# A two-layer network in float32 halves: the last phase's second layers by seven products of mixed blocks

## The chip, the core and the metric

The kernel runs on one core of a Trainium2 chip. The metric is the device time in microseconds of one execution, as the median of several runs; a profile is taken of one execution of its own.

## What is computed

Banded attention (4 batches of 576 positions, 8 heads of 64) gives 2304 tokens of width 512. They pass a mixture of eight experts and then one more two-layer network; the change touches the latter. Cut to what matters:

```python
for e in range(8):                       # phases 0 and 1: experts, F = 1024
    h = np.maximum(x @ w1[e], 0.0)
    out += P[:, e:e + 1] * (h @ w2[e])
...
h = x @ w_in                             # phases 2 and 3: D = 512, F = 2048
r = np.maximum(h, 0.0)
return ((r * r) @ w_out).astype(np.float32)
```

Each float32 operand is kept as a high and a low half in the fast float format, and a product is three matmuls: high by high, low by high and high by low.

## The kernel before

**Steps and phases.** The hidden width is cut in blocks of 256. A step is one such block for one set of tokens, and there are 80: phase 0 is steps 0 to 31 (experts, tokens 0 to 1279), phase 1 steps 32 to 63 (experts, tokens 1280 to 2303), phase 2 steps 64 to 71 (second network, tokens 0 to 1279), phase 3 steps 72 to 79 (second network, tokens 1280 to 2303). `first` holds the starts 0, 32, 64, 72.

**Units.** The instructions of TensorE are written in units of six matmuls of 512 columns. The first layer of step i takes seven of them, u1 to u7, seven products of mixed blocks in place of eight (`l1_pair`, L597; `product`, L533). In phases 0 and 2 a further unit of 24 half-wide matmuls does the tokens 1024 to 1279 (`l1_single`, L698), and two units their second layer. The second layer of step i runs in step i + 1, between the first layer's units: in phases 0, 2 and 3 as eight plain units of 128 tokens (`l2_units`, L722), each ended by an addition into `acc` on VectorE (L755; in the first step of a phase a copy, on VectorE or, for odd c, on ScalarE, L747); in phase 1 (`kept`, L114) as seven products v1 to v7 of mixed blocks of two banks each (`l2_mixed`, L779), whose sums stand with the width, not the tokens, on the partitions. So a step with plain second layer has 15 units in phase 3 and 18 in phase 2, one with a mixed second layer 14.

**What sets the order.** The order on each engine is written out by hand. `after(k, f)` emits f after the unit that stands k units on in the program; I call that slot k of a step. Every engine then works through its own queue in that order, and waits only where data or a buffer are missing; SyncE issues all DMAs in one such queue. The banks of PSUM named mm are three, used in turn.

**Weights.** `prep_w(i)` (L144) splits the first-layer weights of step i + 1 and the second-layer weights of step i. In phase 0 the split weights, and the mixed blocks that VectorE's and GpSimd's sums make of them, are written to DRAM (`store`, L117), and phase 1 fetches them (`fetch`, L121). In phases 2 and 3 the second-layer weights of a step are loaded to the one buffer `raw2` (`load_w`, L138), ScalarE casts the high half (slot 1), VectorE subtracts for the low half (slot 3, L156), and at once the load of the next step's is issued (L228). In step 64 these stand at slots 11 and 13. The first-layer weights go the same way through `raw1` and four GpSimd sums (L170 to L175) with `blk` at slots 2 and 5 and `sum` at slots 8 and 11. Phase 2 also turns the 64-bit input of the second network's weights into float32 (`narrow`, L234) and splits the tokens of phase 3 (`blocks_of`, L273).

**After a unit.** u4's result is copied out of its bank by ScalarE (L677) before u5 may add to that bank.

Of the kernel before, what the change touches and what calls it, by code (L numbers as in the profile page):

```python
# [30 lines left out]
KC = DM // 128  # L31
# [16 lines left out]
def tile_kernel(ctx: ExitStack, tc: tile.TileContext, a):  # L48
# [37 lines left out]
        n + h: dram.tile([NS1 + 1, 128, 1024], F32, name=f"w_{n}{h}") for n in ("blk", "sum", "w2", "mix") for h in ("h", "l")  # L86
# [27 lines left out]
    def kept(i):  # L114
        return NS1 <= i < 2 * NS1
# [28 lines left out]
    def prep_w(i):  # L144
# [52 lines left out]
        if kept(i):  # L197
            w2 = wset[i % 2]["w2"]
            out += [(0, lambda: fetch("w2", i, w2)), (0, lambda: fetch("mix", i, mixes[i % 2]))]
            if i == 2 * NS1 - 3:  # L200
                out += [(2, lambda: load_w(2 * NS1 + 1, 0)), (2, lambda: load_w(2 * NS1, 1))]
        elif 0 <= i < NS1:
            w2 = wset[i % 2]["w2"]
            m = mixes[1]
# [12 lines left out]
            at = (0, 0, 0, 1, 9, 10) if i == 0 else (1, 3, 6, 7, 13, 15)  # L217
            if i:
                out += [(at[0], hi(w2, raw2)), (at[1], lo(w2, raw2, lambda: store("w2", i, w2)))]
            out += [(at[2], m1), (at[3], m2)]  # L220
            out += [(at[4], hi(m, mix32)), (at[5], lo(m, mix32, lambda: store("mix", i, m)))]
        elif i < 0:
# [374 lines left out]
    def l1_pair(i):  # L597
# [7 lines left out]
        def made_here():  # L605
            g_t[i, 0] = tuple(
                z.rearrange("p (f n) -> p f n", f=FC) for z in (gbuf[i % 2][:, :2048], gbuf[i % 2][:, 2048:])
            )
            for n in ("s2", "s3"):
                made[n] = post[0].tile([128, 512], F32, tag=n, name=n, bufs=1)  # L610
            if i == NS1:
                r32.extend((tmp("r1"), tmp("r2"), mix32[:, :512], mix32[:, 512:], tmp("r5")))
# [9 lines left out]
        def out_mixed(fc, t, src, k):  # L622
# [3 lines left out]
            p = p_t[1, steps[i][1] // SPE, t]  # L626
# [58 lines left out]
        def u6():  # L685
            product(bank_b, i, "blk", 3, 3, stop=True)
            out(1, 0, bank_b, 1 if kept(i) else 0)

        def u7():
            product(bank_c, i, "sum", 3, 2, stop=True)  # L690
            after(0, lambda: nc.vector.tensor_tensor(out=made["s2"], in0=bank_c, in1=made["s2"], op=ALU.add))
            out(0, 1, made["s2"], 1 if kept(i) else 2)
# [5 lines left out]
    def l1_single(i):  # L698
        def unit(fcs):

            if fcs[0] == 0:
                g_t[i, 1] = tuple(sg[:, h].rearrange("p (f n) -> p f n", f=FC) for h in range(2))
            gh, gl = g_t[i, 1]
# [18 lines left out]
    def l2_units(i, which):  # L722
# [5 lines left out]
        gh, gl = g_t[i, which]  # L728
# [50 lines left out]
    def l2_mixed(i):  # L779
# [6 lines left out]
        mixed = lambda k: [z[:, k] for z in mix]  # L786
        (a0, a1), (b0, b1) = l2_banks

        def unit(banks, w, n, dst=None, start=False, stop=False, first=False, final=False):
# [11 lines left out]
            def add():  # L801
                e, t = dst
                for m, ps in enumerate(banks):
# [5 lines left out]
                    if final and s == NS1 - 1:  # L809
# [9 lines left out]
            v6=lambda: unit(b_, mixed(1), "t2", (0, 1), first=True),  # L819
            v5=lambda: unit(a_, mixed(0), "t1", (1, 1), start=True, first=True),  # L820
# [369 lines left out]
```

## Time and profile before

| | us |
|---|---|
| median of three runs | 1949.42 |
| the three runs | 1948.12, 1949.42, 1956.59 |
| profiled execution | 1946.08 |
| span of its trace, first to last instruction | 1944.3 |
| phase 2, first unit u1 of step 64 to that of step 72 | 1559.06 to 1772.72 |
| phase 3, first unit u1 of step 72 to the end | 1772.72 to 1944.3 |

Times in the trace count from the first instruction. A busy TensorE is not one at its peak, so a step is measured from the start of its first u1 to that of the next. An engine that is idle costs time only where TensorE waits for it.

### The profile page before, as it was taken

The numbers are of one execution on the slowest core, as the hardware profiler recorded it, in microseconds if no ns is written. First come the engines' busy times: TensorE is split into PE (matmuls) and PEld (weight loads), VectorE is DVE, ScalarE is ACT, GpSimd is POOL, SyncE is SP. The second block draws the span as 40 slices with busy tenths as digits, with TensorE's granted clock in tenths as the row PEclk, the third lists the DMA queues.
The fourth block names the chain that finished last, engine by engine and source line by source line (L and its number), as shares of the span: only waits on it lengthen the run. The fifth ranks groups of instructions, "written<-read, shape, count | busy, mean of one in ns | idle before, by whom it ended". The sixth has DMA issues, their size and how long they took to land.

```text
span 1944.3 us, 29199 instructions
## 1 busy us (share of the span) xinstructions
PE 1926.6 (99%) x11060; PEld 1605.6 (83%) x11060; DVE 1631.1 (84%) x2309; ACT 747.0 (38%) x1222; POOL 601.5 (31%) x532
## 2 busy tenths in 40 slices
PE   8999999999999999999999999999999999999999
PEld 7778888888888888888888888888888878888887
DVE  5867888889888888887589999999999988977776
ACT  3543433333333323333343343433334354433442
POOL 4632333234333322333124243433323331211120
PEclk9999999999999999999999999999999999999999
DMA  7665677676666665666967677675667754334111
GB/s 263 218 239 195 238 269 271 243 275 245 235 250 243 246 244 221 249 225 236 395 238 298 246 261 261 253 256 226 227 229 275 283 198 151 131 125 187 51 54 44
DMA packets 151420, 437.29 MB, mean 225 GB/s; under 512 B 15584, under 2 KB 38512, under 8 KB 151280
## 3 DMA queue, kind: packets, MB, share of 16 engines
q1 hardware_dynamic: 151280, 435.43, 60.4%
q8 instruction: 87, 1.43, 0.3%
q14 instruction: 53, 0.43, 0.1%
HBM read 257.03 MB, written 178.33 MB: 224 GB/s over the span
## 4 chain that ended last, share of the span: by engine, by line
PE 95%; DVE 4%; issue 1%; ACT 1%; POOL 0%; DVEq 0%; ACTq 0%; POOLq 0%
PE mm L738 31%; PE pt L539 16%; PE s L539 11%; PE xt L539 11%; PE mm L794 9%; PE mm L711 6%; PE s L794 3%; PE xt L794 3%; PE xt L412 1%; PE mm L904 1%; PE s L360 1%; PE pt L397 0%; DVE acc L755 0%; DVE suml L156 0%; PE mm L446 0%
## 5 line engine op out<-in xcount | busy, mean ns | idle before, releaser
L738 PE MATMUL mm<-w2h,g 128*128 128x512 f32 x1536 | 474.0, 390 | 0.2 <-DVE acc L749 0.2
L738 PEld LDWEIGHTS mm<-w2h,g 128*128 128x128 f32 x1536 | 287.4, 188 | 59.7 <-DVE acc L749 0.6
L751 DVE SCALAR_TENSOR_TENSOR acc<-mm,ptile,acc 128x512 f32<-128x512 f32 x290 | 216.9, 748 | 103.8 <-PE mm L738 103.5
L738 PE MATMUL mm<-w2l,g 128*128 128x512 f32 x768 | 298.9, 389 | 0.0
L170 POOL TENSOR_TENSOR sums<-raw 128x256 f32<-128x256 f32 x48 | 38.7, 805 | 707.5 <-DVE suml L156 682.4
L738 PEld LDWEIGHTS mm<-w2l,g 128*128 128x128 f32 x768 | 144.2, 188 | 30.2
L640 POOL TENSOR_TENSOR r<-mix,r 128x512 f32<-128x512 f32 x32 | 42.2, 1318 | 408.0 <-DVE mix L629 396.1
L619 DVE TENSOR_TENSOR g<-r,g 128x512 fp32r<-128x512 f32 x128 | 147.6, 1153 | 12.8 <-ACT g L616 4.6
L755 DVE TENSOR_TENSOR acc<-mm,acc 128x512 f32<-128x512 f32 x146 | 99.3, 687 | 56.9 <-PE mm L738 56.0
L539 PE MATMUL pt<-x_hi,sumh 128*128 128x512 f32 x320 | 124.8, 390 | 1.3 <-ACT s L677 1.3
L539 PE MATMUL s<-x_hi,blkh 128*128 128x512 f32 x320 | 125.4, 392 | 0.6 <-ACT pt L665 0.6
L539 PE MATMUL xt<-x_hi,sumh 128*128 128x512 f32 x320 | 125.0, 391 | 0.0
L539 PE MATMUL xt<-x_hi,suml 128*128 128x512 f32 x320 | 124.7, 390 | 0.1
L616 ACT CAST g<-mix 128x512 fp32r<-128x512 f32 x96 | 59.7, 622 | 169.5 <-DVE mix L629 103.2
L539 PE MATMUL s<-x_lo,blkh 128*128 128x512 f32 x320 | 124.7, 390 | 0.0
L577 ACT ACTIVATE sg<-mm 128x512 fp32r<-128x512 f32 (+1 forms) x35 | 19.7, 562 | 273.1 <-PE mm L711 273.1
L539 PE MATMUL s<-x_hi,blkl 128*128 128x512 f32 x320 | 124.6, 389 | 0.0
L539 PE MATMUL pt<-x_lo,sumh 128*128 128x512 f32 x320 | 124.5, 389 | 0.0
L539 PE MATMUL pt<-x_hi,suml 128*128 128x512 f32 x320 | 124.5, 389 | 0.0
L539 PE MATMUL xt<-x_lo,sumh 128*128 128x512 f32 x320 | 124.5, 389 | 0.0
L808 DVE TENSOR_TENSOR acc<-mm,acc 128x512 f32<-128x512 f32 x188 | 120.2, 680 | 0.0
L711 PE MATMUL mm<-xs,blkh 128*128 128x256 f32 x640 | 115.8, 280 | 0.0
(202 smaller groups left out, 4646.1 us busy)
## 6 DMA issues: line engine op xcount, KB each, us to landing
raw<-in_w SPq DMA_DIRECT2D x61, 512.0 KB, 5.8
w_blkh<-blkh SPq DMA_DIRECT2D x33, 512.0 KB, 6.1
w_blkl<-blkl SPq DMA_DIRECT2D x33, 512.0 KB, 6.5
w_sumh<-sumh SPq DMA_DIRECT2D x33, 512.0 KB, 6.7
w_suml<-suml SPq DMA_DIRECT2D x33, 512.0 KB, 2.6
blkh<-w_blkh SPq DMA_DIRECT2D x33, 512.0 KB, 3.3
blkl<-w_blkl SPq DMA_DIRECT2D x33, 512.0 KB, 4.2
sumh<-w_sumh SPq DMA_DIRECT2D x33, 512.0 KB, 4.5
```

The lines of the kernel that those rows point to most:

```text
L170: tt(out=c(sums, 0), in0=c(raw1, 2), in1=c(raw1, 3), op=ALU.add)
L539: nc.tensor.matmul(ps, w[:, c], z[:, x, j], start=start and k == 0, stop=stop and k == 5, skip_group_check=True)
L577: after(k, lambda: nc.scalar.activation(out=ghi, in_=src, func=AF.Relu))
L616: after(k, lambda: nc.scalar.copy(b[:, 0], src))
L619: lambda: nc.vector.tensor_tensor(out=b[:, 1], in0=src, in1=b[:, 0].bitcast(F32), op=ALU.subtract),
L640: sub = lambda o, x, y: nc.gpsimd.tensor_tensor(out=o, in0=x, in1=y, op=ALU.subtract)
L711: nc.tensor.matmul(ps[:, n * NSG:n * NSG + NSG], w[:, c], z[:, kc], start=k == 0, stop=k == 3 * KC - 1)
L738: nc.tensor.matmul(ps, g[:, fc, c * 128:c * 128 + 128], wt[:, fc], start=k == 0, stop=k == 3 * FC - 1)
L751: nc.vector.scalar_tensor_tensor(out=dst, in0=ps, scalar=p, in1=dst, op0=ALU.mult, op1=ALU.add)
L755: nc.vector.tensor_tensor(out=dst, in0=ps, in1=dst, op=ALU.add)
L794: nc.tensor.matmul(ps, w[wt][:, c], z[:, g], start=start and k == 0, stop=stop and k == 2, skip_group_check=True)
L808: nc.vector.tensor_tensor(out=o, in0=ps, in1=o, op=ALU.add)
```

## The change

The second layers of steps 72 to 78 go by seven products of mixed blocks, as in phase 1. For that, phase 2 writes the split weights of its steps to DRAM: `blk`, `sum`, `w2`, and the four mixed blocks of `w2`. The mixed blocks are made in place in `raw2` by four GpSimd sums (m3, m4), their high half goes to a buffer of its own, their low half back to `raw2`, both are stored from there, and only then is the next step's `raw2` loaded. Phase 3 fetches all this in place of loading and splitting weights. The weight cast of step 65 moves from slots 1 and 3 to 9 and 11; in steps 66 to 71 it stays at 1 and 3. The relu of two of the four blocks is written out by ScalarE first, and VectorE's product follows one slot later. The second layer of step 79 stays plain. As the sums of phase 3 now stand turned, 32 transposes (eight sets of four) turn them back between its eight units.

```diff
     def kept(i):
-        return NS1 <= i < 2 * NS1
+        return NS1 <= i < 2 * NS1 or i >= first[3]
+
+    def mixed(i):
+        return kept(i) and i < len(steps) - 1
+
+    def place(i):
+        return i % NS1 if i < first[2] else NS1 + (i - first[2]) % NS2
 
...
-        if NS1 < n <= 2 * NS1:
+        if NS1 < n <= 2 * NS1 or first[3] <= n < len(steps):
...
             def keep(name):
                 if n == 0:
                     kept_back.append(lambda: store(name, 0, w[name]))
-                elif n <= NS1:
-                    store(name, n, w[name])
+                else:
+                    store(name, NS1 if n == NS1 else place(n), w[name])
...
         if kept(i):
             w2 = wset[i % 2]["w2"]
-            out += [(0, lambda: fetch("w2", i, w2)), (0, lambda: fetch("mix", i, mixes[i % 2]))]
+            out += [(0, lambda: fetch("w2", i, w2))]
+            if mixed(i):
+                out += [(0, lambda: fetch("mix", i, mixes[i % 2]))]
...
+            def m3():
+                tt(out=r[:, 1, 1], in0=r[:, 0, 1], in1=r[:, 1, 1], op=ALU.add)
+                tt(out=r[:, 0, 1], in0=r[:, 0, 0], in1=r[:, 0, 1], op=ALU.subtract)
+
+            def m4():
+                tt(out=r[:, 0, 0], in0=r[:, 1, 1], in1=r[:, 0, 0], op=ALU.subtract)
+                tt(out=r[:, 1, 0], in0=r[:, 1, 0], in1=r[:, 0, 0], op=ALU.subtract)
+
+            if moe:
+                at = (0, 0, 0, 1, 9, 10) if i == 0 else (1, 3, 6, 7, 13, 15)
+            else:
+                at = {first[2]: (11, 13, 14, 14, 19, 20), first[2] + 1: (9, 11, 12, 12, 16, 17)}.get(i, (1, 3, 4, 5, 9, 11))
             if i:
-                out += [(at[0], hi(w2, raw2)), (at[1], lo(w2, raw2, lambda: store("w2", i, w2)))]
+            if moe:
+                out += [(at[2], m1), (at[3], m2)]
+                out += [(at[4], hi(mixes[1], mix32)), (at[5], lo(mixes[1], mix32, lambda: store("mix", place(i), mixes[1])))]
+            elif i + 1 < first[3]:
+                m = (mixes[1][0], raw2.bitcast(F32R))
+
+                def mix_done():
+                    store("mix", place(i), m)
+                    load_w(i + 1, 1)
+
+                out += [(at[2], m3), (at[3], m4), (at[4], hi(m, raw2)), (at[5], lo(m, raw2, mix_done))]
...
-        else:
-            w = wset[i % 2]
-            at = (11, 13) if late else (1, 3)
-            out += [(at[0], hi(w["w2"], raw2)), (at[1], lo(w["w2"], raw2, lambda: load_w(i + 1, 1)))]
...
+            if i == len(steps) - 1:
+                pair = {(0, 0): block["11"], (1, 1): block["21"], (1, 0): block["t2"], (0, 1): block["t1"]}
+                g_t[i, 0] = {k: (z[:, 0], z[:, 1]) for k, z in pair.items()}
...
-            p = p_t[1, steps[i][1] // SPE, t]
+            moe = steps[i][0]
+            if moe:
+                p = p_t[1, steps[i][1] // SPE, t]
+            elif (fc, t) in ((0, 0), (1, 0)):
+                p = post[0].tile([128, T], F32, tag="pp", name="pp", bufs=3)
+                after(k, lambda: nc.scalar.activation(out=p, in_=src, func=AF.Relu))
+                k += 1
+            else:
+                p = src
             after(
                 k,
                 lambda: nc.vector.scalar_tensor_tensor(
@@ -631,11 +666,11 @@
                 ),
             )
             if (fc, t) == (0, 0):
-                operand("11", g, 1, 2)
+                operand("11", g, k + 1, k + 2)
...
             elif (fc, t) == (1, 0):
-                operand("21", g, 2, 3)
+                operand("21", g, k + 1, k + 2)
...
             k = 0
+            t, c0 = divmod(c, T // 128)
             for fc in range(FC):
+                gh, gl = g_all[fc, t]
                 for g, wt in ((gh, whi), (gl, whi), (gh, wlo)):
                     nc.tensor.matmul(
-                        ps, g[:, fc, c * 128:c * 128 + 128], wt[:, fc], start=k == 0, stop=k == 3 * FC - 1
+                        ps, g[:, c0 * 128:c0 * 128 + 128], wt[:, fc], start=k == 0, stop=k == 3 * FC - 1
                     )
                     k += 1
+            if i == len(steps) - 1:
+                o, ch = by_token[c], t0 // 128 + c
+
+                def add():
+                    nc.vector.tensor_tensor(out=o, in0=ps, in1=o, op=ALU.add)
+                    nc.sync.dma_start(out[ch * 128:(ch + 1) * 128], o)
+
+                after(1 if c == 0 else 0, add)
+                return
...
+        if i == len(steps) - 1:
+            d = acc[0].rearrange("p (k t n) -> p k t n", k=KC, t=2)
+            flat = [z.rearrange("p b c -> p (b c)") for z in (raw1, sums)] + [raw2, mix32]
+            by_token = [z[:, h * DM:h * DM + DM] for z in flat for h in range(2)]
+
+            def by_tokens(c):
+                ps = bank("s")
+                t, c0 = divmod(c, T // 128)
+                for kc in range(KC):
+                    nc.tensor.transpose(
+                        ps[:, kc * 128:kc * 128 + 128], d[:, kc, t, c0 * 128:c0 * 128 + 128], ident
+                    )
+                nc.scalar.copy(by_token[c], ps)
+
+            units, turns = ([lambda c=c, f=f: f(c) for c in range(2 * T // 128)] for f in (unit, by_tokens))
+            return [units[0], turns[0]] + [u for k in range(1, len(units)) for u in (turns[k], units[k])]
+
...
+        places = range(4) if steps[i][0] else (3, 0, 1, 2)
+        mixed_w = lambda k: [z[:, places[k]] for z in mix]
...
-            l2 = [] if kept(i - 1) else l2_units(i - 1, 0)
+            l2 = [] if mixed(i - 1) else l2_units(i - 1, 0)
...
+            if i in (NS1 + 1, first[3] + 1):
                 s0, s1 = bank("s"), bank("s")
...
-                elif i == first[2] - 1:
+                elif i in (first[2] - 1, len(steps) - 1):
                     names = "u1 v1 u2 v2 u3 u4 v6 u5 v5 u6 u7 v7 v3 v4"
...
-                    after(min(k, len(order) - 1), f)
+                    after(k if k > 18 else min(k, len(order) - 1), f)
...
-                splits.append(blocks_of(2, y_dram[:, :, PAIRS[1]:], y1 + two(mixes[1][0])))
+                splits.append(blocks_of(2, y_dram[:, :, PAIRS[1]:], y1 + two(mixes[1][1])))
```

## Rows read from the trace of the kernel before

**Rows 1.** Page, part 1: an engine's busy time, share of the span, instructions.

```profile
PE 1926.6 (99%) x11060; PEld 1605.6 (83%) x11060; DVE 1631.1 (84%) x2309; ACT 747.0 (38%) x1222; POOL 601.5 (31%) x532
```

**Rows 2.** Windows by step: length, busy by engine, clock, DMA share, GB/s.

```profile
1516.82:1535.86 19.04, 19.04 (x85) 15.77 (x84) 17.28 (x26) 6.96 (x12) 6.31 (x4) 1.00 0.58 221
1578.26:1605.65 27.39, 26.59 (x127) 21.83 (x126) 24.85 (x32) 15.28 (x25) 10.82 (x10) 1.00 0.43 157
...
1631.94:1657.92 25.98, 25.98 (x128) 21.99 (x127) 23.38 (x37) 11.40 (x18) 3.65 (x4) 1.00 0.47 152
...
1684.17:1710.15 25.98, 25.98 (x128) 21.99 (x127) 24.95 (x36) 11.88 (x19) 7.52 (x8) 1.00 0.38 132
1710.15:1737.21 27.06, 26.28 (x129) 21.92 (x127) 21.13 (x31) 10.84 (x17) 3.66 (x4) 1.00 0.22 69
...
1807.16:1827.56 20.40, 20.40 (x92) 16.89 (x90) 13.85 (x20) 9.46 (x15) 3.21 (x4) 1.00 0.15 51
```

**Rows 3.** Timeline of PE between phases 0 and 1: start, length, instruction.

```profile
939.18 0.60 PE L767 MATMUL mm<-ident,acc 128*128 128x128 f32 x4
939.53 0.70 PE L738 MATMUL mm<-w2h,g 128*128 128x512 f32 x2
...
940.99 0.60 PE L767 MATMUL mm<-ident,acc 128*128 128x128 f32 x4
```

**Rows 4.** Timeline of ACT in steps 65 and 68.

```profile
1591.81 0.62 ACT L280 CAST mixh<-mix 128x512 fp32r<-128x512 f32 x1
...
1594.36 0.59 ACT L747 COPY acc<-mm 128x512 f32<-128x512 f32 x1
...
1660.49 1.06 ACT L152 CAST w2h<-raw 128x1024 fp32r<-128x1024 f32 x1
...
1663.57 0.59 ACT L677 COPY s<-pt 128x512 f32<-128x512 f32 x1
```

**Rows 5.** Timeline of PE, u5 of steps 68 and 70; in brackets the wait.

```profile
1664.73 0.39 PE L539 MATMUL pt<-x_hi,sumh 128*128 128x512 f32 x1
...
1717.91 0.50 PE L539 MATMUL pt<-x_hi,sumh 128*128 128x512 f32 x1 [0.78 <-ACT s L677]
```

**Rows 6.** Timeline of DVE in steps 64, 65 and 67.

```profile
1576.80 1.22 DVE L156 TENSOR_TENSOR w2l<-raw,w2h 128x1024 fp32r<-128x1024 f32 x1
...
1587.40 1.22 DVE L156 TENSOR_TENSOR blkl<-raw,blkh 128x1024 fp32r<-128x1024 f32 x1
...
1598.46 1.21 DVE L156 TENSOR_TENSOR suml<-sums,sumh 128x1024 fp32r<-128x1024 f32 x1
...
1649.99 1.22 DVE L156 TENSOR_TENSOR suml<-sums,sumh 128x1024 fp32r<-128x1024 f32 x1
```

**Rows 7.** Timeline of POOL, step 69: first and last of four sums.

```profile
1703.58 0.73 POOL L170 TENSOR_TENSOR sums<-raw 128x256 f32<-128x256 f32 x1 [15.46 <-DVE suml L156]
...
1706.23 1.07 POOL L175 TENSOR_TENSOR sums<-raw,sums 128x256 f32<-128x256 f32 x1
```

**Rows 8.** Timeline of SP's DMA issues in phase 0.

```profile
647.20 0.32 SPq L119 DMA_DIRECT2D w_suml<-suml  x1
...
649.16 0.32 SPq L119 DMA_DIRECT2D w_mixl<-mixl  x1
```

**Rows 9.** DMA issues, 645 to 655 us: size, median us from issue to landing.

```profile
w_suml<-suml SPq DMA_DIRECT2D x1, 512.0 KB, 2.6
w_mixh<-mixh SPq DMA_DIRECT2D x1, 512.0 KB, 3.6
w_mixl<-mixl SPq DMA_DIRECT2D x1, 512.0 KB, 5.0
```

**Rows 10.** DMA issues, 1577 to 1579.5 us, same columns.

```profile
raw<-w SPq DMA_DIRECT2D x1, 512.0 KB, 3.3
```

**Rows 11.** DMA issues, 656 to 668 us, beside seven other transfers.

```profile
raw<-in_w SPq DMA_DIRECT2D x2, 512.0 KB, 6.1
...
w_w2l<-w2l SPq DMA_DIRECT2D x1, 512.0 KB, 6.2
```

More of the change, by code (lines that the diff above doesn't have):

```diff
@@ L85, in tile_kernel @@
     w_dram = {
-        n + h: dram.tile([NS1 + 1, 128, 1024], F32, name=f"w_{n}{h}") for n in ("blk", "sum", "w2", "mix") for h in ("h", "l")
+        n + h: dram.tile([NS1 + NS2, 128, 1024], F32, name=f"w_{n}{h}") for n in ("blk", "sum", "w2", "mix") for h in ("h", "l")
     }
@@ L605, in made_here @@
         def made_here():
[L606 to L608 removed]
+            if i == len(steps) - 1:
+                pair = {(0, 0): block["11"], (1, 1): block["21"], (1, 0): block["t2"], (0, 1): block["t1"]}
+                g_t[i, 0] = {k: (z[:, 0], z[:, 1]) for k, z in pair.items()}
+            else:
+                gh, gl = (z.rearrange("p (f n) -> p f n", f=FC) for z in (gbuf[i % 2][:, :2048], gbuf[i % 2][:, 2048:]))
+                g_t[i, 0] = {(f, t): tuple(z[:, f, t * T:t * T + T] for z in (gh, gl)) for f in range(FC) for t in range(2)}
             for n in ("s2", "s3"):
                 made[n] = post[0].tile([128, 512], F32, tag=n, name=n, bufs=1)
[L611 to L612 removed]
+            if i in (NS1, first[3]):
+                r32[:] = (tmp("r1"), tmp("r2"), mix32[:, :512], mix32[:, 512:], tmp("r5"))
         def operand(n, src, k, k_lo):
@@ L686, in u6 @@
             product(bank_b, i, "blk", 3, 3, stop=True)
-            out(1, 0, bank_b, 1 if kept(i) else 0)
+            out(1, 0, bank_b, 1 if mixed(i) else 0)
         def u7():
@@ L691, in u7 @@
             after(0, lambda: nc.vector.tensor_tensor(out=made["s2"], in0=bank_c, in1=made["s2"], op=ALU.add))
-            out(0, 1, made["s2"], 1 if kept(i) else 2)
+            out(0, 1, made["s2"], 1 if mixed(i) else 2)
             if steps[i][0] and steps[i][1] % SPE == SPE - 1:
@@ L698, in l1_single @@
     def l1_single(i):
+        whole = []
         def unit(fcs):
             if fcs[0] == 0:
-                g_t[i, 1] = tuple(sg[:, h].rearrange("p (f n) -> p f n", f=FC) for h in range(2))
-            gh, gl = g_t[i, 1]
+                whole[:] = [sg[:, h].rearrange("p (f n) -> p f n", f=FC) for h in range(2)]
+                g_t[i, 1] = {(f, 0): tuple(z[:, f] for z in whole) for f in range(FC)}
+            gh, gl = whole
             ps = (spare[0] if i == 2 * NS1 else bank("mm"))[:, :len(fcs) * NSG]
@@ L808, in add @@
                         nc.vector.tensor_tensor(out=o, in0=ps, in1=o, op=ALU.add)
-                    if final and s == NS1 - 1:
+                    if final and steps[i][0] and s == NS1 - 1:
                         t0 = PAIRS[1] + t * T
@@ L818, in l2_mixed @@
             v2=lambda: unit(a_, whole(1, 0), "21", (0, 0), stop=True, first=True, final=True),
-            v6=lambda: unit(b_, mixed(1), "t2", (0, 1), first=True),
-            v5=lambda: unit(a_, mixed(0), "t1", (1, 1), start=True, first=True),
-            v7=lambda: unit(b_, mixed(2), "t3", (1, 1), final=True),
-            v3=lambda: unit(a_, mixed(3), "22", (0, 1), stop=True, final=True),
+            v6=lambda: unit(b_, mixed_w(1), "t2", (0, 1), first=True),
+            v5=lambda: unit(a_, mixed_w(0), "t1", (1, 1), start=True, first=True),
+            v7=lambda: unit(b_, mixed_w(2), "t3", (1, 1), final=True),
+            v3=lambda: unit(a_, mixed_w(3), "22", (0, 1), stop=True, final=True),
             v4=lambda: unit(b_, whole(1, 1), "t4", (1, 0), stop=True, first=True, final=True),
@@ L1042, in tile_kernel @@
                 ahead, l2, l2s = l2[:len(l2) - 3] + l2s, l2[len(l2) - 3:], []
-            if i == NS1 + 1:
+            if i in (NS1 + 1, first[3] + 1):
                 s0, s1 = bank("s"), bank("s")
                 x0, x1 = bank("xt"), bank("xt")
-                own.update((k, (s0, bank_p, x0)) for bank_p in [bank("pt")] for k in range(i, 2 * NS1))
-                l2_banks.extend(((bank("mm"), bank("mm")), (s1, x1)))
+                until = 2 * NS1 if i < 2 * NS1 else len(steps)
+                own.update((k, (s0, bank_p, x0)) for bank_p in [bank("pt")] for k in range(i, until))
+                l2_banks[:] = ((bank("mm"), bank("mm")), (s1, x1))
                 spare.append(bank("mm"))
@@ L1051, in tile_kernel @@
             l1s = l1_single(i) if pair_of(i) == 0 else []
-            if kept(i - 1):
+            if mixed(i - 1):
                 v = l2_mixed(i - 1)
```

21 lines of the change are left out of this document (8 added, 13 removed).

## Prediction

> **What bounds the kernel now.** I read the page's busy shares first, then windows cut at the steps. TensorE is busy 99% of the span [rows 1], and in the steps of phases 1 and 3 a window is as long as its PE busy time, at full clock [rows 2]: 19.04 us for a mixed step of 14 units, 20.40 us for a plain one of 15, so 1.36 us a unit. Phase 2 is the place with little room: a step there is 25.98 us with VectorE busy 23.4 to 25.0 of it, and the first and one late step have lost 1.4 and 1.1 us already (27.39 and 27.06 against 25.98) [rows 2]. So a unit less in phase 3 is worth its full 1.36 us, and anything late in phase 2 is seen at once. Nothing can be won beyond the units removed and the few microseconds that phase 2 loses today.
>
> **Part 1, phase 3.** The second layers of seven steps, 72 to 78, go from eight units to seven. These run in steps 73 to 79: 7 x 1.36 = 9.52 us less. I take the whole of it, since the mixed step of phase 1 has the same DMA fetches, adds and GpSimd sums and runs at 19.04 us with VectorE busy 17.28 and ScalarE 6.96 [rows 2]. Phase 3 adds two relus of about 0.6 us to ScalarE, which has 12 us free, and moves two products on VectorE a slot later; I put that at nothing. If that cover fails, it is a rival (E). The preparation of weights that leaves phase 3 is worth nothing, since VectorE was busy 13.85 of 20.40 us there.
>
> **Part 2, the turning back.** Eight sets of four transposes stand between the last eight units. Phase 0's end shows the same form: from the set at 939.18 to the unit at 939.53 is 0.35 us, and that unit takes until 940.99, 1.46 us in place of 1.36 [rows 3]. So 0.45 us a set, 3.6 us in all. The ScalarE copies (0.59 us each, as those of L747 [rows 4]) and two banks keep pace with one set per 1.8 us. The tail behind the last unit (one addition, one DMA) stays. Sum of parts 1 and 2: -9.52 + 3.6 = -5.9 us.
>
> A set of four costs 0.45 us, so one costs 0.11 us [rows 3]. The Trainium skill, page "TensorE: Matmul & The Clock Gate", section "Part 4: PE-mode transpose", gives some 275 ns for one in a kernel; by an estimate from that figure 32 would be 8.8 us and the sum of these two parts -0.7 us. The row is of the same instruction in this kernel, so I keep 3.6.
>
> **Part 3, phase 2: a loop through one buffer.** This decides. Before, `raw2` is free as soon as VectorE has subtracted the low half (slot 3). Now it is cast, subtracted, mixed by four GpSimd sums, cast again, subtracted again at slot 11, stored, and only when that store has landed does SyncE issue the load of the next step's weights. ScalarE meets that load at slot 1 of the next step, and what is queued behind the cast on ScalarE is the copy of u4's bank, without which u5 can't start.
>
> *The deadline.* In step 68, begun at 1657.92, the cast starts at 1660.49, the copy ends at 1663.57 + 0.59 = 1664.16, u5 starts at 1664.73 [rows 4, 5]. So the cast may be 0.57 us late: it must start by 3.14 us into the step. Step 70 shows what comes else: u5 waited 0.78 us for that copy [rows 5].
>
> *The loop in a settled step.* In step 67, begun at 1631.94, `sum`'s subtraction starts 18.05 us in and ends at 19.27 [rows 6]. The GpSimd sums new in this step take 3.7 us for four, by the row of 1703.58 to the end of that at 1706.23 [rows 7], and VectorE pays for them: step 69 with POOL at 7.52 us has VectorE at 24.95, step 67 with 3.65 has 23.38 with a like count of instructions, 1.6 us for 3.9 [rows 2]. That is for a full overlap; before slot 11 I take 1.0 us (bounds 0 and 3.7). So the store of `suml` goes out about 20.3 us in, then those of `mixh` and, 1.2 us later, `mixl`. Phase 0 issues these three in the same order within 2 us: from `suml` at 647.20 to the landing of `mixl` at 649.16 + 5.0 is 7.0 us [rows 8, 9]. A load on an emptied queue lands after 3.3 us [rows 10]. 20.3 + 7.0 + 3.3 = 30.6 us, and the next step begins at 25.98, so the weights are there 4.6 us into it: 1.5 us after the deadline. Steps 68, 69 and 70 pay this; 67 about 0.5, since the stall of step 66 has let VectorE catch up with the units; 71 about 1.0, since step 70 has little narrowing (VectorE 21.13 us [rows 2]). That is 6.0 us, less the 1.1 us that step 70 loses today at the same copy: 4.9. Bounds: nothing, if stores land in the 2.6 us of one alone [rows 9]; 5 us a step if store and load take 6.2 and 6.1 us as in the fullest stretch of phase 0 [rows 11].
>
> *Step 65.* It starts late in the loop: step 64's mixed blocks are subtracted at slot 5 of step 65, ahead of the `blk` subtraction that now starts at 1587.40; that is 1.2 us, where the weight subtraction of slot 3 has gone, so about 1589 [rows 6]. Store alone 2.6, load 3.3 [rows 9, 10]: 1595. ScalarE reaches the cast at slot 9 at 1592.4 (the end of the row at 1591.81), waits to 1595 and then casts, so the copy out of the bank at 1594.36 is some 3.6 us later [rows 4]. Three banks give 2.7 us of room; the rest and VectorE's own delay make about 2.0 us, between 0 and 6.
>
> *Step 66.* The low half of step 65's weights then comes behind `sum`'s subtraction (1598.46, now 1.6 us later, and 1.2 long [rows 6]) and is done near 1602.4; four sums of 1 us, a cast of 1.05, a subtraction of 1.2: 1608.7; mixed-store landing 3.1 (between 2.6 and 3.6), load 3.3: 1615.1. Step 66 begins near 1607.7, its deadline is 1610.8, so TensorE waits about 4.3 us (0 to 9).
>
> Phase 2 in all: 2.0 + 4.3 + 4.9 = 11.2 us more. Other additions there are at nothing: eight stores of 512 KB per step into a queue busy 0.38 to 0.47 of the time [rows 2] (a full queue is rival C), and ScalarE's extra cast of 1.05 us with half its time free.
>
> **Sum.** -5.9 + 11.2 = +5.3 us. On the profiled execution, 1946.08: 1951.4. The median of the runs shown, 1949.42, lies 3.3 us above that execution, so I give 1955.
>
> **Rivals.**
> A, the forecast: the loop through `raw2` misses its deadline by a little in most steps, 1955 (1949 to 1961).
> B, the weights are back in time: hidden. Landings at the short end, 2.6 and 3.3 us, remove the wait in steps 67 to 71 and most of steps 65 and 66, and the 1 to 3 us that phase 2 loses today may go too. For it: the queue is half empty. Against it: three stores stand before the load. -5.9 + 1.5 = -4.4, 1945 (1939 to 1948).
> C, slower: the round trip is longer, because the stores of `w2`, `blk` and `sum` share the queue. From the fullest stretch [rows 11] half the excess over my values, 2 us a step in seven steps: +14, 1969. It turns the sign beyond what I call no change when the round trip is 0.6 us longer than I took in each of the seven.
> D, VectorE becomes the bound in steps 65 to 69: it is busy 24.95 of 25.98 us in step 69 and gets 1.2 us and up to 3.9 us of collision with GpSimd [rows 2]; 1.5 us more in five steps, +7: 1962. In the Trainium skill, page "SBUF — State Buffer", section "Who interferes with whom", a VectorE instruction with two inputs in SBUF and a GpSimd one that reads SBUF lock each other out whole; by an estimate from the rule four sums of 0.9 us would cost 3.7 us a step. The rows show 1.6 for 3.9, so half of it at most.
> E, phase 3 does not reach 19.04 us a step, because the relu of u6 and the product behind it come a slot later: half the gain is gone, +4.8: 1960.
>
> **Chances.** A 0.45, B 0.25, C 0.15, D 0.10, E 0.05. The likeliest gives 1955. For 8 in 10 the range must hold A, nearly all of B and half of C and D: 1943 to 1967. What a measurement here can tell from no change is about 0.5%, 9.7 us: faster (under 1939.7) only at the low end of B, 0.04; slower (over 1959.1): C, half of D and E, a fifth of A, 0.31; within, 0.65. The gain's ceiling, 5.9 us and 3 of today's waits, is why "faster" is so small.
>
> **What would show it.** Right: steps 73 to 79 at 19.04 us; eight gaps of 0.45 us in the last eight units; u5 of step 66 waiting 3 to 5 us and of steps 68 to 70 1 to 2 us, each for the copy at ScalarE behind a cast that a DMA released. Wrong: the cast of slot 1 without idle time before it (B); landings over 6 us for `mixl` (C); TensorE waiting for VectorE's additions rather than ScalarE's copy (D); steps over 19.1 us in phase 3 (E).

## The result and the profile after

| | before | after |
|---|---|---|
| median of the runs, us | 1949.66 (1945.92 to 1956.59) | 1961.90 (1959.39 to 1963.71) |
| profiled execution, us (its span) | 1946.08 (1944.3) | 1962.93 (1961.2) |

The ratio is 1.0061, 95% interval 1.0042 to 1.0079: 12 us slower, where 1955 was forecast (1943 to 1967). The page's first part shows TensorE with 10 instructions fewer than in [rows 1] and 98% busy instead of 99%:

```profile
PE 1928.1 (98%) x11050; PEld 1602.0 (82%) x11050; DVE 1660.0 (85%) x2337; ACT 747.1 (38%) x1238; POOL 647.0 (33%) x556
```

Windows of steps 65 to 70 and of two steps of phase 3, columns as in [rows 2]:

```profile
1581.63:1616.02 34.39, 28.19 (x127) 22.97 (x126) 25.13 (x32) 17.19 (x27) 15.95 (x15) 0.95 0.89 328
1616.02:1647.77 31.75, 28.19 (x128) 22.98 (x127) 27.20 (x37) 12.70 (x20) 15.23 (x14) 0.95 0.74 263
1647.77:1674.68 26.91, 26.27 (x128) 21.91 (x127) 24.90 (x38) 12.02 (x19) 7.85 (x8) 1.00 0.79 288
1674.68:1702.04 27.36, 26.56 (x129) 21.85 (x128) 25.19 (x36) 12.65 (x20) 10.10 (x9) 1.00 0.81 286
1702.04:1729.32 27.28, 26.53 (x129) 21.82 (x128) 26.15 (x36) 12.73 (x20) 12.90 (x12) 1.00 0.79 287
1729.32:1756.84 27.52, 26.58 (x129) 21.84 (x128) 23.14 (x33) 11.48 (x18) 4.13 (x4) 1.00 0.57 226
1825.51:1844.55 19.04, 19.04 (x86) 15.77 (x85) 17.32 (x24) 8.77 (x16) 6.63 (x4) 1.00 0.62 219
1844.55:1864.09 19.54, 19.33 (x85) 15.69 (x84) 18.91 (x26) 7.91 (x14) 6.32 (x4) 1.00 0.59 216
```

Step 65 took 27.39 us before and step 67 25.98 [rows 2]. The DMA share (last column but one), 0.38 to 0.47 in steps 65 to 69 of [rows 2], is now 0.74 to 0.89 in steps 65 to 69. TensorE's idle times, from its timeline (start, length, instruction, in brackets the wait ahead of it): one row each of step 65, step 66, a settled step of phase 2 and a step of phase 3.

```profile
1605.98 1.05 PE L776 MATMUL mm<-w2h,g 128*128 128x512 f32 x2 [5.05 <-ACT acc L794]
1626.07 0.50 PE L563 MATMUL pt<-x_hi,sumh 128*128 128x512 f32 x1 [3.08 <-ACT s L710]
1668.98 0.73 PE L776 MATMUL mm<-w2h,sg 128*128 128x512 f32 x2 [0.64 <-DVE acc L802]
1871.49 0.50 PE L859 MATMUL s<-g,mixh 128*128 128x512 f32 x1 [0.21 <-DVE g L646]
```

The terms of the sum, forecast and measured (lengths from a step's first matmul to the next step's):

| term | forecast | measured |
|---|---|---|
| step 65 | +2.0 | 34.39 - 27.39 = +7.0 |
| step 66 | +4.3 | 31.75 - 26.29 = +5.5 |
| steps 67 to 71 | +4.9 | +0.9, +1.1, +1.3, +0.5, 0 = +3.8 |
| steps 73 to 79 | -9.5 | 135.90 - 143.24 = -7.3 |
| last eight units | +3.6 | 15.14 - 10.65 = +4.5 |
| sum | +5.3 | +13.4 |

The two profiled executions differ by 16.85 us. 3.35 of it lie ahead of step 0, in code that is the same, and 0.1 behind the last unit. Such differences ahead of the change are in every single execution (step 64 starts between 1557 and 1569 us), so the experiments are read by their steps and not by their totals; each but the last is one execution. Of the twelve runs of the last, e12, one took 3223 us at a mean granted clock of 0.555 and is left out of its ratio.

### The profile page after: what moved, and what is told of

The parts are those of the page before. It is cut to its first block, busy times and chain, and to the rows that moved or that the text cites. A ratio compares the mean times of both kernels' runs of the same rounds, so it can differ in the third digit from the quotient of the medians.

```text
span 1961.2 us, 29450 instructions
## 1 busy us (share of the span) xinstructions
PE 1928.1 (98%) x11050; PEld 1602.0 (82%) x11050; DVE 1660.0 (85%) x2337; ACT 747.1 (38%) x1238; POOL 647.0 (33%) x556
## 4 chain that ended last, share of the span: by engine, by line
PE 88%; DVE 8%; ACT 1%; issue 1%; DMA 1%; POOL 0%; DVEq 0%; ACTq 0%; POOLq 0%
PE mm L776 26%; PE pt L563 16%; PE s L563 10%; PE xt L563 10%; PE mm L859 10%; PE mm L747 5%; PE s L859 4%; PE xt L859 4%; DVE g L646 2%; PE xt L436 1%; PE mm L969 1%; DVE acc L873 1%; PE s L384 1%; DVE acc L802 1%; PE pt L421 0%
## 5 line engine op out<-in xcount | busy, mean ns | idle before, releaser
L776 PE MATMUL mm<-w2h,g 128*128 128x512 f32 x1312 | 407.7, 392 | 5.1 <-ACT acc L794 5.1
L776 PEld LDWEIGHTS mm<-w2h,g 128*128 128x128 f32 x1312 | 246.1, 189 | 56.0 <-ACT acc L794 5.5
L776 PE MATMUL mm<-w2l,g 128*128 128x512 f32 x656 | 256.2, 391 | 0.0
L675 POOL TENSOR_TENSOR r<-mix,r 128x512 f32<-128x512 f32 x39 | 51.8, 1328 | 551.8 <-DVE mix L664 539.8
L646 DVE TENSOR_TENSOR g<-r,g 128x512 fp32r<-128x512 f32 x156 | 182.0, 1169 | 14.2 <-ACT g L643 5.4
L873 DVE TENSOR_TENSOR acc<-mm,acc 128x512 f32<-128x512 f32 x226 | 144.6, 677 | 1.8 <-PE mm L859 1.8
L776 PEld LDWEIGHTS mm<-w2l,g 128*128 128x128 f32 x656 | 123.7, 189 | 26.0
L643 ACT CAST g<-mix 128x512 fp32r<-128x512 f32 x117 | 72.7, 622 | 187.3 <-DVE mix L664 108.5
L601 ACT ACTIVATE g<-s 128x512 fp32r<-128x512 f32 x96 | 59.6, 621 | 137.0 <-DVE s L715 69.5
```

The costliest lines, as they stand in the source:

```text
L601: after(k, lambda: nc.scalar.activation(out=ghi, in_=src, func=AF.Relu))
L643: after(k, lambda: nc.scalar.copy(b[:, 0], src))
L646: lambda: nc.vector.tensor_tensor(out=b[:, 1], in0=src, in1=b[:, 0].bitcast(F32), op=ALU.subtract),
L675: sub = lambda o, x, y: nc.gpsimd.tensor_tensor(out=o, in0=x, in1=y, op=ALU.subtract)
L776: nc.tensor.matmul(ps, g[:, c0 * 128:c0 * 128 + 128], wt[:, fc], start=k == 0, stop=k == 3 * FC - 1)
L873: nc.vector.tensor_tensor(out=o, in0=ps, in1=o, op=ALU.add)
```

## Experiments

Steps in us, and in the last column steps 73 to 79 together:

| run | 65 | 66 | 67 | 68 | 69 | 70 | 65 to 70 | 73 to 79 |
|---|---|---|---|---|---|---|---|---|
| before | 27.39 | 26.29 | 25.98 | 26.25 | 25.98 | 27.06 | 158.95 | 143.24 |
| after | 34.39 | 31.75 | 26.91 | 27.36 | 27.28 | 27.52 | 175.21 | 135.90 |
| e1 load first | 28.12 | 31.74 | 26.92 | 27.38 | 27.29 | 27.55 | 169.00 | 135.82 |
| e2 no sums | 28.68 | 28.12 | 26.76 | 27.30 | 26.80 | 27.53 | 165.20 | 135.89 |
| e3 block slot | 34.97 | 32.34 | 26.90 | 27.38 | 27.31 | 27.48 | 176.38 | 133.95 |
| e5 turn order | 35.23 | 32.06 | 26.89 | 27.36 | 27.31 | 27.48 | 176.33 | 135.89 |
| e6 two buffers | 29.51 | 29.47 | 27.52 | 27.37 | 27.72 | 29.14 | 170.73 | 135.82 |
| e7 slot 15 | 30.05 | 28.31 | 26.80 | 26.30 | 28.80 | 31.29 | 171.55 | 135.89 |
| e7b slot 9 | 29.32 | 29.99 | 27.17 | 27.94 | 27.21 | 29.27 | 170.90 | 135.82 |
| e8 all four | 29.02 | 28.71 | 26.81 | 26.25 | 28.84 | 29.71 | 169.34 | 133.97 |
| e9 early chain | 30.55 | 27.38 | 26.90 | 27.37 | 27.28 | 27.56 | 167.04 | 135.88 |
| e10 square | 30.92 | 28.16 | 27.64 | 28.16 | 28.16 | 27.65 | 170.69 | 133.93 |
| e11 slots | 28.21 | 26.63 | 26.84 | 26.41 | 27.45 | 29.79 | 165.33 | 133.94 |
| e12 best | 28.25 | 26.64 | 26.76 | 26.44 | 26.94 | 27.56 | 162.59 | 133.97 |

**e1, the load ahead of the store.**

```diff
-                m = (mixes[1][0], raw2.bitcast(F32R))
+                m = (mixes[1][0], mixes[0][0])
                 def mix_done():
-                    store("mix", place(i), m)
                     load_w(i + 1, 1)
+                    store("mix", place(i), m)
```

> The load of the next step's second-layer weights no longer waits for the store of the mixed pieces: their low half goes to a free buffer, and the load is issued ahead of that store. Theory (store and load in series through one buffer cause the long idle times of TensorE): the 5.05 us in step 65 and the 3.08 us in step 66 fall below 1 us each, the granted clock stays at 1.00 behind them, step 65 takes about 28 us and step 66 about 27, steps 67 to 70 stay at 26.9 to 27.5 because VectorE sets them; 1951 us in all. Rival (a full DMA queue, not the order): the load itself then lands after 6 us or more, TensorE still idles over 2 us in step 65, about 1957. Rival (the prediction's cast at slot 1 in steps 67 to 70): these steps fall to about 26.0 as well, 1946.

In the changed kernel the chain of step 65 reads as follows: issue of the store, its landing in the rows of DMA issues (last number, us), issue of the load, and the cast on ScalarE that waits for it; the copy that empties TensorE's bank stands behind that cast.

```profile
1592.54 0.32 SPq L125 DMA_DIRECT2D w_mixl<-raw  x1
...
w_mixl<-raw SPq DMA_DIRECT2D x1, 512.0 KB, 6.7
...
1599.28 0.80 SPq L144 DMA_DIRECT2D raw<-w  x2
...
1603.36 1.04 ACT L158 CAST w2h<-raw 128x1024 fp32r<-128x1024 f32 x1 [5.91 <-DMA raw<-w]
```

With the load first, the same cast and the wait of u5 in step 66:

```profile
1596.04 1.06 ACT L158 CAST w2h<-raw 128x1024 fp32r<-128x1024 f32 x1 [0.78 <-DMA raw<-w]
...
1617.71 0.80 PE L563 MATMUL pt<-x_hi,sumh 128*128 128x512 f32 x1 [3.15 <-ACT s L710]
```

Step 65: the idle 5.05 us are gone and the step is 6.3 us shorter; the theory holds there, and the full queue alone makes a short wait only (the load took 5.6 us, and the cast waited 0.78). Step 66: the theory fails, 31.74 against 31.75. The mixed subtraction of step 65 now ends 2.27 us into step 66 (1609.84), where in the changed kernel it ends 0.4 us in, because the stall of step 65 had let the chain catch up; so the 2.6 us of the store's landing that e1 takes out of the chain are lost again, by its later start (1.9 us) and a load that lands after 4.3 us in place of 3.4. Steps 67 to 70 do not move at all, so what they lose has nothing to do with the load.

**e2, GpSimd's sums left out**, on top of e1 (the calls of `m3` and `m4` removed).

> As the run before, but GpSimd's four sums of the second-layer weights in phase 2 are left out, so that the mixed pieces stored are not mixed; the two casts and two subtractions remain. Theory (VectorE is slowed by GpSimd's sums beside it): steps 67 to 70 fall by about 1 us each to 25.98 to 26.3, VectorE's busy time per step by 1.0 to 1.6 us; some 4 us less than the run before. Rival (VectorE's own second subtraction of 1.2 us is the cause): steps 67 to 70 stay within 0.3 us of the run before.

Steps 67 to 70 lose only 0.16, 0.08, 0.49 and 0.02 us, and the wait in front of the single's unit stays (0.48, 0.74 and 0.49 us in steps 67 to 69). Step 67 in e1 and in e2, columns as in [rows 2] (VectorE's busy time is 24.90 and 24.13 us, GpSimd's 7.86 and 4.58):

```profile
1639.31:1666.22 26.91, 26.28 (x128) 21.92 (x127) 24.90 (x38) 12.02 (x19) 7.86 (x8) 1.00 0.79 285
```

```profile
1634.57:1661.33 26.76, 26.28 (x129) 21.92 (x128) 24.13 (x38) 12.11 (x19) 4.58 (x4) 1.00 0.80 282
```

VectorE's busy time falls by 0.77 us and the step by 0.16; in steps 68 to 70 VectorE's falls by 0.51, 0.32 and 1.08. So the collision is there, smaller than expected, and it is not what sets most of these steps; in step 69 it may be a part of it. Step 66, with a chain shorter by four sums, goes to 28.12: it is the length and start of the chain that makes step 66 late.

**e6, e7, e7b: a buffer for the raw weights, and the slot of the subtraction.** In e6, from step 65 on, the load goes to `mixes[0][0]`, the sums read it and write `raw2`, and the next load is issued right behind the sums; step 65's cast is back at slot 1. e7 moves the mixed subtraction of steps 66 to 70 from slot 11 to 15, e7b to 9 (the cast to 7).

```diff
+        if which and i > first[2]:
+            dst = mixes[0][0].bitcast(F32)
...
-                tt(out=r[:, 1, 1], in0=r[:, 0, 1], in1=r[:, 1, 1], op=ALU.add)
+                tt(out=q[:, 1, 1], in0=r[:, 0, 1], in1=r[:, 1, 1], op=ALU.add)
...
+                if i > first[2]:
+                    load_w(i + 1, 1)
```

> From step 65 on the raw second-layer weights go to a buffer of their own, and the four sums read it and write the old one, so the next load waits for the sums alone and no longer for cast, subtraction and store of the mixed pieces; step 65's cast is back at slot 1. Theory (step 66 is late because the load for it waits for the end of step 65's late chain, not for the queue): the idle time of 3.1 us in step 66 goes, and the low clock behind it; step 65 takes 27.4 to 28.1 us, step 66 26.3 to 27.3, steps 67 to 70 stay at 26.9 to 27.5; about 1950 us. Rival (VectorE has too much work around step 66): step 66 stays over 29 us, with TensorE waiting for VectorE; about 1953.

> As the run before, and in steps 66 to 70 the subtraction of the mixed pieces stands at slot 15 in place of 11, where the subtraction of the sums stands too. Theory (two subtractions of 1.2 us back to back in one slot make an addition late, and with it a bank of TensorE): the idle times of 0.48, 0.64, 0.80 and 0.75 us in steps 67 to 70 go, these steps take 26.0 to 26.4 us and step 70 about 27.0; some 3 us less than the run before. Rival (VectorE has no room left in these steps, wherever the subtraction stands): the idle times come back at another unit and the steps stay at 26.9 to 27.5.

> As the run with two buffers, and in steps 66 to 70 the cast of the mixed pieces stands at slot 7 and their subtraction at slot 9, ahead of that of the sums at 11. Theory (only the same slot is the trouble): steps 67 to 70 at 26.0 to 26.4 us as with slot 15. Rival (VectorE is still behind at slot 11 when it has done one more subtraction since slot 6): the idle times stay at 0.5 to 0.8 us.

All three fell short: 170.7 to 171.6 us for the six steps, against 169.0 in e1. e6's step 66 (29.47, with waits of 1.05, 0.73 and 0.77 us) is on its rival's side. e7b takes the single's wait away in steps 66 to 69 but has another of 0.55 us, for an addition, in step 68 (27.94). But the three separate two things. VectorE's rows in step 67 of the changed kernel, ahead of the wait of 0.64 us at 1668.98:

```profile
1665.98 1.22 DVE L162 TENSOR_TENSOR suml<-sums,sumh 128x1024 fp32r<-128x1024 f32 x1
1667.11 1.22 DVE L162 TENSOR_TENSOR raw<-raw,mixh 128x1024 fp32r<-128x1024 f32 x1
1668.24 0.68 DVE L802 TENSOR_TENSOR acc<-mm,acc 128x512 f32<-128x512 f32 x1
```

Two subtractions of slot 11 stand back to back, and the addition that frees the bank comes behind both. With slot 15 that wait is gone in all of steps 66 to 69 (steps 67 and 68 at 26.80 and 26.30). (The four waits of 0.48, 0.64, 0.80 and 0.75 us that the expectations name are those of steps 66 to 69; step 70 waits 0.93 us at u5, as before with 0.78 [rows 5].) In its place u5 waits in steps 69 and 70 for ScalarE's copy, which stands behind a cast that waited for VectorE. In e7's step 70 (begun at 1722.56), first TensorE's row, then GpSimd's first sum, then one of VectorE's operations of the narrowing, and below it the same sum and the same operation in e1's step 70 (begun at 1720.90):

```profile
1732.93 0.50 PE L570 MATMUL pt<-x_hi,sumh 128*128 128x512 f32 x1 [3.39 <-ACT s L717]
...
1724.94 0.74 POOL L229 TENSOR_TENSOR raw<-mixh 128x256 f32<-128x256 f32 x1 [5.00 <-DMA w_mixl<-raw]
...
1726.00 1.11 DVE L295 SCALAR_TENSOR_TENSOR xb<-xb 128x512 f32<-128x512 uint32 x1
```

```profile
1727.64 0.73 POOL L226 TENSOR_TENSOR raw<-raw 128x256 f32<-128x256 f32 x1 [9.46 <-DVE w2l L162]
...
1722.68 0.69 DVE L288 SCALAR_TENSOR_TENSOR xb<-xb 128x512 f32<-128x512 uint32 x1
```

In e1 the sums write over what the low half reads, so GpSimd has to wait for that subtraction; with a buffer of its own GpSimd no longer waits for it, and its sums meet the narrowing that decides the start of the step. Taking a wait from GpSimd moved its work to a worse place. The buffer is only a part of it: in step 70 u5 waits 0.92 us in e1, 2.56 in e6 with the subtraction still at slot 11, and 3.39 in e7.

**e9, step 64's chain early**, on top of e1.

```diff
-                at = {first[2]: (11, 13, 14, 14, 19, 20), first[2] + 1: (9, 11, 12, 12, 16, 17)}.get(i, (1, 3, 4, 5, 9, 11))
+                at = {first[2]: (6, 7, 7, 7, 10, 13)}.get(i, (1, 3, 4, 5, 9, 11))
```

> As the run with the load ahead of the store, and step 64 casts, subtracts and sums its second-layer weights at slots 6 and 7 and the mixed pieces at 10 and 13, in the idle time that VectorE and GpSimd have there; so step 65's weights are loaded at slot 13 of step 64 as in the kernel before, and step 65 keeps to the slots of the later steps. Theory (step 66's 3.1 us come from the late start of the chain in step 64, handed on from step to step): the idle time in step 66 falls below 1 us with no low clock behind it, step 65 takes 27.4 to 28.1 us, step 66 26.3 to 27.3; steps 67 to 70 stay at 26.9 to 27.5. Rival (VectorE sets steps 65 and 66 as well, so an earlier chain only moves the wait): the two together stay over 57 us, as they did with two buffers (59.0).

Step 66 is at 27.38 without an idle row at u5: its wait was the late start of the chain, handed on from step 64. Step 65 is worse than expected (30.55: 1.59 us at u5 and 0.95 at the single's unit), since its cast, at slot 1 again and so ahead of u4's copy, waited 1.93 us for the load. The two are 57.9 together, over the 57 that the rival named: a part of the wait did move, from step 66 to step 65.

**e10, squares on ScalarE**, on top of e9 and with the edits of e3 and e5: g = Square(relu) in place of VectorE's product for three of the four blocks in phase 2.

> As the run before, with the edits of phase 3 and of the turns that each stood alone; and in phase 2 three of the five squares of a step are made by ScalarE from its own relu instead of by VectorE's product, some 2.0 us off VectorE per step. Theory (VectorE's work just ahead of the single unit sets steps 67 to 70): their idle times of 0.5 to 0.8 us go, these steps take 26.0 to 26.4 us, step 70 up to 27.0; phase 3's steps at 19.04; 12 us or more below the changed kernel and 4 to 7 below the kernel before. Rival (it is the two subtractions back to back that make one addition late, however little VectorE has to do ahead of them): the idle times stay.

The rival was right, and more than that: the waits grew.

```profile
1689.06 0.68 DVE L805 TENSOR_TENSOR acc<-mm,acc 128x512 f32<-128x512 f32 x1
1689.66 1.21 DVE L162 TENSOR_TENSOR suml<-sums,sumh 128x1024 fp32r<-128x1024 f32 x1
1690.79 1.22 DVE L162 TENSOR_TENSOR mixh<-raw,mixh 128x1024 fp32r<-128x1024 f32 x1
...
1692.66 0.72 PE L779 MATMUL mm<-w2h,sg 128*128 128x512 f32 x2 [1.22 <-DVE acc L805]
```

VectorE now had idle times of 1.83 and 0.77 us, waiting for casts that ScalarE made later, and the pair of subtractions came 19.4 us into step 68 (begun at 1670.22), in the changed kernel 18.7. So less work on VectorE did not shorten these steps. As ScalarE was slower here too, e10 alone doesn't show that the order in front of one addition sets them; e7 and e11 do.

**e11 and e12, the slots alone**, on e9 (and so e1), with e3 and e5: the mixed subtraction at slot 13 in place of 11, two slots behind the other; in e11 step 65's cast at slot 5, behind u4's copy, and its mixed subtraction at 14, in e12 also those of steps 69 and 70. The line of e12:

```diff
+                at = {64: (6, 7, 7, 7, 10, 13), 65: (5, 7, 8, 8, 12, 14), 69: (5, 7, 8, 8, 12, 14), 70: (5, 7, 8, 8, 12, 14)}.get(i, (1, 3, 4, 5, 9, 13))
```

> The load ahead of the store (in-place sums as in the changed kernel), step 64's chain early, step 65's cast at slot 5 (behind the copy that its fifth unit needs) with the mixed subtraction at 14, and in steps 66 to 70 the mixed subtraction at slot 13, two slots behind that of the sums; phase 3's earlier block and the order of the turns; squares as in the changed kernel. Theory (what delays a bank is two subtractions back to back, and what delays a cast is where it stands, not the amount of VectorE's work): steps 67 to 70 at 26.0 to 26.5 us (70: 27.0), step 65 about 28, step 66 about 26.7, so steps 65 to 70 take some 161 us against 158.95 before and 175.2 in the changed kernel; about 4 us below the kernel before. Rival (VectorE has no room, and the wait comes back as a late copy at the fifth unit, as with slot 15 and two buffers): steps 69 and 70 at 28 us or more, the six steps over 165.

> As the run before, with steps 69 and 70 laid out like step 65 (cast of the second-layer weights at slot 5, behind the copy that the fifth unit waits for; mixed subtraction at 14). Theory (the copy is late because the cast of 1.05 us stands ahead of it on ScalarE): the idle times of 0.64 us in step 69 and 1.85 us in step 70 fall by about 1 us, so that neither has a low clock behind it; step 69 about 26.8, step 70 about 27.6, steps 65 to 70 together 162 to 163 us. Rival (VectorE is late for the single's product as well, so that the cast is not what decides): step 70 stays over 29. In all 118.2 and less in steps 73 to 78 plus the turns: 3 to 4 us below the kernel before, a ratio of 0.998; at worst 1.000.

e11: there is no wait in front of the single's unit in steps 66 to 70 any more, and steps 65 to 68 come nearly as the theory has them; step 69 waits 0.64 us at u5, and step 70 is the rival's, with u5 1.85 us late, as are the six steps together (165.33). e12: with the cast behind the copy, step 69 is 26.94 and step 70 27.56. The 1.29 us that u5 still waits in step 70 are VectorE's, as the rival has it: another cast ahead of that copy waited 3.01 us for the product of the single's unit, behind the narrowing. The six steps take 162.59 us, 12.6 less than in the changed kernel and 3.6 more than before. From step 65 to the end e12 is 1.4 us shorter than the kernel before, by these two executions, where 3 to 4 us were expected; the measured ratio is 1.0002 (0.9990 to 1.0013; medians 1947.54 of 12 runs and 1946.95 of 17). The change, repaired, is worth nothing that can be measured. Step 67 still takes 0.78 us more than before without an idle time of 0.15 us or more on TensorE; where that goes is not shown.

**e3, phase 3's block one slot earlier.**

```diff
-            out(1, 0, bank_b, 1 if mixed(i) else 0)
+            out(1, 0, bank_b, 1 if mixed(i) and steps[i][0] else 0)
```

> In phase 3 the relu, product, cast and subtraction of hidden block (1, 0) come one slot earlier, where phase 1 has them. Theory (the low half of that block now falls beside GpSimd's sums, 1.78 us in place of 0.68, and makes the low halves of the mixed blocks late): steps 75 to 78 go from 19.54 to 19.59 back to 19.04, about 2.5 us in all, 1959.5. Rival (the slower low halves have another cause, such as the pair of relus): the 0.2 us idle in each step stays, 1961.9.

Steps 74 to 79 at 19.04 each; 1.95 us for the seven steps, where 2.5 were expected. The low half of that block in the changed kernel, beside GpSimd's sum (POOL, its second of four), and in e3, ahead of it:

```profile
1865.86 1.63 POOL L675 TENSOR_TENSOR r<-r,r 128x512 f32<-128x512 f32 x1
...
1866.26 1.78 DVE L646 TENSOR_TENSOR g<-mix,g 128x512 fp32r<-128x512 f32 x1
```

```profile
1861.30 0.68 DVE L646 TENSOR_TENSOR g<-mix,g 128x512 fp32r<-128x512 f32 x1
```

The subtraction ends at 1868.04, 0.55 us behind the end of GpSimd's sum at 1867.49. The Trainium skill, page "SBUF — State Buffer", section "Who interferes with whom", says that such a VectorE instruction with two inputs in SBUF is blocked whole while GpSimd reads there; this row agrees within 0.13 us, as 1867.49 and its own 0.68 would make 1868.17.

**e5, the order of the turns.**

```diff
-                after(1 if c == 0 else 0, add)
+                after((3, 3, 3, 3, 0, 1, 1, 0)[c], add)
...
+            u, t = units, turns
+            return [u[0], t[4], u[1], t[0], u[2], t[1], u[3], t[2], u[4], t[3], u[5], t[5], u[6], t[6], t[7], u[7]]
```

> In the tail the first set of transposes is that of a token group whose sums were done earlier, and a unit stands between it and the next set. Theory (the first two sets of turns wait for the last additions of the step before): the last eight units with their turns take 14.9 us in place of 15.6, with 0.35 us a set and 0.10 us on the unit behind it; 0.7 us less, 1961.2. Rival (the wait comes back at a later set, for a bank that ScalarE's copy frees): 15.6, no change.

Windows over the last eight units with their turns, changed kernel and then e5:

```profile
1941.85:1957.20 15.35, 15.00 (x81) 12.01 (x79) 7.81 (x12) 5.22 (x9) 0.00 (x0) 1.00 0.27 104
```

```profile
1942.81:1957.40 14.59, 14.59 (x81) 12.00 (x79) 7.81 (x12) 5.22 (x9) 0.00 (x0) 1.00 0.29 110
```

To the start of the last matmul it is 14.36 us against 15.14, and 10.65 before: the turns cost 3.7 us, where 8 x 0.45 is 3.6, and the rest was the first two sets waiting for the additions of v4.

**e8, e7 with e3 and e5.**

> The four edits together: the buffer of its own, slot 15, the earlier block of phase 3 and the order of the turns. If each takes away what it took away alone, the sum is about 1950 - 3 - 2.6 - 0.8 = 1943.6 us, 6 us below the kernel before; if VectorE has no room in phase 2, about 1947.

Phase 3 added up (133.97), phase 2 did not (169.34): the repairs of phase 2 were not yet the right ones.

## Why the prediction was right or wrong

The range held the time and the sign of the sum was right, but the median came 7 us above the forecast, at 0.61% slower in place of the "within 0.5%" that had the largest chance, and of the five terms the mechanism was right in three: steps 65 and 66 and the price of the turns.

- **Step 65 (+2.0, measured +7.0): right in mechanism, wrong in size.** The store was forecast for about 1589; it was issued at 1592.54, which is 1589.2 when the 3.35 us ahead of step 0 are taken off. The failing step is the landing: 2.6 us from the row of one store alone [rows 9], 6.7 in fact, and 4.1 for the load in place of 3.3 [rows 10]. Of the 7.0 us, 5.05 are the idle time and 1.6 the lower clock behind it (below), for which the sum had no term. I had put the eight stores per step at nothing, by a queue that was 0.4 busy as a mean over the step [rows 2]. The mean hid fuller stretches: in the same step of the kernel before, 6.7 us stood at 0.88 (first line, share in the last column but one). In the changed kernel the queue was at 1.04 and 1.01 up to the store:

```profile
1585.80:1592.50 6.70, 6.70 (x31) 5.57 (x30) 4.49 (x7) 4.37 (x7) 0.00 (x0) 1.00 0.88 314
```

```profile
1581.60:1585.80 4.20, 3.06 (x14) 2.21 (x13) 4.10 (x6) 1.92 (x4) 3.96 (x4) 1.00 1.04 410
1585.80:1592.50 6.70, 6.70 (x30) 5.53 (x31) 5.27 (x7) 5.17 (x8) 4.19 (x5) 1.00 1.01 342
```

And the 3.3 us of the load was the shortest of nine weight loads in phase 2 of the kernel before, which landed after 3.3 to 5.4 us, 4.4 in the middle. Rival C's "full queue" was right here and only here: e1 shows that the wait also needs store and load in series.

- **Step 66 (+4.3, measured +5.5): right in mechanism; the size is in part luck.** The chain was late, as forecast, with a store landing after 2.6 us and a load after 3.4 (3.1 and 3.3 forecast). The idle time was 3.08 us where 4.3 was forecast, and 1.9 us of TensorE's lower clock behind it (below), which the sum did not have, made up for that. e1 and e9 show that the late start of the chain decides here, and not the order of store and load.

- **Steps 67 to 71 (+4.9, measured +3.8): wrong in mechanism.** The round trip was forecast at 7.0 + 3.3 us from the issue of `suml`'s store; in step 67 it took 1667.22 to 1672.32 and then 3.4, that is 8.5 us, so the weights were there 1.0 us into the next step (begun at 1674.68), well ahead of the cast, which has no wait in its row:

```profile
1667.22 0.32 SPq L125 DMA_DIRECT2D w_suml<-suml  x1
...
1672.32 0.32 SPq L144 DMA_DIRECT2D raw<-w  x1
...
1677.26 1.05 ACT L158 CAST w2h<-raw 128x1024 fp32r<-128x1024 f32 x1
```

This is rival B's sign, the cast without idle time before it. What came late was an addition on VectorE behind two subtractions in one slot, which the prediction placed at slot 11 itself and priced at nothing. This is nearest to rival D in its place (VectorE), but not in its cause: e2 shows that GpSimd's new sums are worth 0.02 to 0.49 us a step, and e7 and e11 that the slot takes the wait away. That the size came near is luck.

- **Phase 3 (-9.5, measured -7.3): rival E in its place, at less than half its size (2.2 us for 4.8).** The product one slot later was put at nothing under the cover of phase 1's window; the cover was the time before GpSimd's sums begin. e3 gives 1.95 us of the missing 2.2 back; the rest lies in step 73 (19.73 us in e12, with a wait of 0.35).

- **The turns (+3.6, measured +4.5): the price of a set right.** The wait of the first two sets for the last step's additions was missing from the sum; e5 takes 0.78 us of it away.

In the repaired kernel e12 the terms read: steps 73 to 79 -9.27, turns +3.71, steps 65 to 70 +3.64, the end behind the last unit +0.54, together -1.38. So the ceiling of 5.9 us for phase 3 and the turns was nearly reached (5.56), and phase 2 still pays 3.64 of it back with its long waits gone.

## What to carry to other kernels

A landing time belongs to the queue as it will be, not as it is: when a change itself adds stores, price the first step in which they pile up with the fullest stretch that the trace has, and look whether a load stands behind one of them. On an engine that is 90% busy, look at which instructions will stand in one slot ahead of the one that frees a bank, before adding up busy times: moving one subtraction by two slots took the waits away that less work and a further buffer had not. A slot is only as good as what runs beside it; moving work by one slot, or taking a wait away, can bring two engines together that a dependency had kept apart.

## What the runs showed of the hardware

The price of the long idle times was more than the idle time. Windows right behind an idle time of TensorE, of the changed kernel (5.05 us), of e11 (1.85 us) and of e12 (1.29 us); the granted clock is the last column but two:

```profile
1605.90:1609.50 3.60, 3.52 (x9) 2.75 (x10) 3.60 (x5) 1.66 (x4) 0.25 (x1) 0.54 1.04 416
```

```profile
1723.66:1727.16 3.50, 3.50 (x11) 2.75 (x12) 3.50 (x4) 1.05 (x2) 3.04 (x3) 0.67 0.96 384
```

```profile
1723.40:1726.90 3.50, 3.50 (x15) 2.92 (x16) 3.05 (x5) 2.01 (x3) 0.00 (x0) 1.00 0.72 288
```

The length of the idle time alone does not decide this. Behind 2.56 us in e6 the clock stayed up (line below), and behind 2.76 in e7b too; and an idle time of 1.94 us at the end of phase 1 was followed by 1.00 in e7b and by 0.66 in e5. So steps with such a wait (e6, e7, e7b and e11 in step 70) can differ by the clock as well as by the wait.

```profile
1735.66:1739.16 3.50, 3.50 (x15) 2.92 (x16) 3.05 (x5) 1.06 (x2) 0.00 (x0) 1.00 0.98 393
```

Behind 5.05 us TensorE ran near the lower of its two levels (1.2 of 2.4 GHz) for some 3.6 us: 9 matmul instructions counted in the window against 15. In steps 65 and 66 PE's busy time is 28.19 us, 1.6 and 1.9 more than before (26.59 and 26.29). I had no such term; two stalls of 8.1 us together cost 3.5 more.

The tail's 32 transposes between matmuls ran at a granted clock of 1.00. The Trainium skill, page "TensorE: Matmul & The Clock Gate", section "Part 4: PE-mode transpose", says that the full clock does not come on for them; in this stretch, where they are a few between many matmuls, it did not fall, and a set of four took 0.35 us.
